# Attention with sinks and windows, then a gated long convolution, on one core: a third of the transform table copied by sign, turns as integers, the first evacuations in halves, and a new written-out order

## The chip, the cores and the metric

The kernel runs on one core of one Trainium2 chip. The metric is the device time of one execution in microseconds (us): 197.66 us is the median of three runs of the kernel before (197.52 to 197.74). A core has a matrix engine (PE), a vector engine (DVE), a scalar engine (ACT), GpSimd (POOL) and SyncE (SP), which here does nothing but issue DMAs. Each engine has an instruction queue of its own and takes it in order. PSUM holds what PE writes; here it is four pairs of banks, called slots 0 to 3.

## The reference

```python
def _attn_ref(q, k, v, is_retrieval, n_sink, window):     # 4 x 8 heads, 768 positions, head size 64
    scores = scale * np.matmul(q, k.transpose(0, 1, 3, 2))
    ...                                    # retrieval heads: causal; the others: causal and (sink or window of 64)
    scores = np.where(mask[None, :, :, :], scores, -1000000000.0)
    a = np.exp(scores - np.max(scores, axis=-1, keepdims=True))
    a = a / (np.sum(a, axis=-1, keepdims=True) + 1e-09)
    return np.matmul(a, v)

def _moe_ref(x, w_proj, filter_fft, w_out):               # x: 4 x 768 x 512, the heads side by side
    proj = x @ w_proj
    x1, x2, x3 = proj[..., :D], proj[..., D:2 * D], proj[..., 2 * D:]
    X2 = np.fft.rfft(x2, n=S, axis=1)
    H = np.fft.rfft(filter_fft, n=S, axis=0)[None, :, :]
    x2_conv = np.fft.irfft(X2 * H, n=S, axis=1)
    return (x1 * x2_conv * x3) @ w_out
```

## The kernel before

The 32 heads are worked on as 16 pairs `n` (four pairs for each of the four batches `b`). The transform is done as matmuls with a table `G` of cosines and sines, over 384 frequencies in three segments of 128 columns (segment 2 holds 64 cosines and 64 sines of the upper frequencies); `Gi` is its transpose.

Nothing is scheduled by a compiler. Each step is a small function under a name, and the string `ORDER` at the head of the file lists the names one after another; that list is the order of every engine's queue, the DMA issues of SP included. `@2` behind a name gives the PSUM slot, `/v`, `/s` and `/p` send a step that several engines can do to DVE, ACT or POOL. A step waits on semaphores for its inputs and for the buffer that it overwrites, and everything behind it on its engine waits too.

The names that matter here:

- `lq lk lv`: loads of a pair's q, k, v (L515, L527; 384 KB each, three buffers each). `cq ck cv`: casts to bf16. `T`: transposes, on PE for pairs 0 to 5 (L550), by DMA for pairs 6 to 15 (L560). `E`: copies PE's transposes out of PSUM into `qkT`.
- `sc n.c`: scores of chunk `c` (L574), `ex`: their exponentials on ACT (L593). `CHUNKS` says which 128 x 128 blocks (key block, query block) make a chunk. The two heads of a pair lie on partitions 0 to 63 and 64 to 127, so a score matmul uses half the rows of the array. `sb`: a bias added by a matmul, for the first four pairs (L587); the others are masked on DVE (`mk`, L603).
- `vf`: a masked copy of v (`v_far`, L541). `at`: probabilities times v (L612). `rec`, `nm`: normalization on DVE (L622, L627).
- `f`, `S`, `Se`: the two half sums, the transform (L640) and its copy out of PSUM. `tn`, `te`: the turned attention output (`xT`).
- `X`, `Xe`, `pa pb pc`: projection of the spectrum (L681) and its product with the filter; `c`, `ce`, `cv b.cb`: the inverse transform (L742); `x1`, `x3`, `xs`, `g`, `y`: the other two projections (L717) and the gates; `o`, `oe`, `st`: the output projection (L769), its copy and its store. `lw0 lw1 lw2` and `lwo`: weight loads, issued on POOL (L414, L419). `lw1` is the part that `X` reads.
- The table: `turns`, `angle`, `wrap` turn position times frequency into a fraction of a turn between -1/2 and 1/2 (three DVE steps for each of three row blocks, 384 columns wide); `size` takes its magnitude; `sin1 sin2 cos1 cos2` write `G` on ACT; `sin0` loads the sine's table ahead. `blank` are matmuls on zeros before there is work. `lret`, `heads0` to `heads2`: which heads are of which kind. `alt` writes one column of `G` on POOL.

The casts, copies and the steps in the table have one helper each, so many instructions carry the helper's line (L180 DVE, L182 POOL, L184 ACT).

Of the kernel before, what the change touches and what calls it, by code (L numbers as in the profile page):

```python
# [19 lines left out]
    [(0, 0), (0, 1), (0, 2), (0, 3)],  # L20
    [(4, 4), (4, 5), (0, 4), (0, 5)],
    [(1, 1), (1, 2), (1, 3), (1, 4)],
    [(3, 3), (3, 4), (3, 5)],
# [23 lines left out]
sc3.0@3 sc3.3@2 f02/v sb3.0 vf3/v sb3.3 ex3.0 T4.1@0 scales T4.0 F2.0 ck5/p E4.1/v ex3.3 S2.0@3 cq6/p H2.2/s
E4.0/v S2.1 at3.1@2 H2.0/s Se2/v tn2@0 at3.0 H2.1/s te2/v cv4/p sc4.1@3 rec3 lq7 sc4.2@0 nm3 F0.1@1 ex4.2
F0.0 f03/v ex4.1 f13/v tn3@0 cq5/v T5.1@2 H0.0/v T5.0 S3.0@3 te3/v E5.0/s S3.1 H0.2/v E5.1/s x10.0.0@0
H0.1/v Se3/s x10.0.1 H0.3/v x10.1.0@2 H0.4/v xs0.0/s cv5/p lv6 kinds sc4.3@3 sc4.0@1 ex4.3 sc5.1@0 x10.1.1  # L50
ex4.0 mask1 x30.0.0@3 xs0.1/v lk8 ex5.1 x30.0.1 mask0 sc4.5@2 g0.0 sc4.4@1 ex4.5 X0.1.0@0 ex4.4 mask2 mk4.1
sc5.0@3 sc5.2@2 ex5.0 sc5.4@1 mk4.0 X0.1.1 mask6 ex5.2 x10.3.1@3 Xe0.1/v vf5/s x10.3.0 ck6/p F1.1@2 xs0.3/v
ex5.4 F1.0 T6 mask3 sc5.5@3 vf4/v H1.0/s sc5.3@1 cq7/p x30.1.0@0 mk4.2 lq8 ex5.5 x30.1.1 lv7 ex5.3 X0.2.1@3
mk5.2 H1.1/s at4.1@1 mk5.0 H1.2/s X0.2.0 ck7/s mk5.1 g0.1 cv6/s at4.0 T7 Xe0.2/s at5.1@2 mask4 vf6/p rec4
at5.0 nm4 ck8/s sc6.4@3 rec5 sc6.2@0 f04/v ex6.4 lq9 x10.2.0@1 nm5 x10.2.1 lk9 ex6.2 mask7 mask5 sc6.5@2
cq8/p sc6.1@3 xs0.2/v ex6.5 x30.2.0@0 ex6.1 f15/p mk6.2 sc6.0@1 sc6.3@2 T8 x30.2.1 ex6.0 X0.0.0@3 f05/v
ex6.3 g0.2 sc7.3@1 sc7.1@2 mk6.0 ex7.3 sc7.5@0 X0.0.1 mk6.1 ex7.5 tn4 f14/v S4.0@1 ex7.1 cv7/v sc7.4@0
Xe0.0/v tn5 vf7/p S4.1 ex7.4 S5.1@2 Se4/v cq9/p sc7.0@3 sc7.2@0 ex7.0 S5.0 ck9/v at6.1@1 mk7.2 ex7.2 T9
at6.0 mk7.0 Se5/s sc8.4@3 mk7.1 sc8.0@0 hB ex8.0 rec6 at7.0@2 sw0.1 nm6 sw0.0 at7.1 ex8.4 hA f06/v f16/p
sc8.5@0 lv8 sc8.3@1 rec7 ex8.5 S6.0@3 tn6 nm7 ex8.3 sc8.2@0 S6.1 f17/v ex8.2 f07/v tn7 S7.1@1 Se6/v S7.0  # L60
pa0.1 sc9.2@0 Se7/s sc9.4@3 lk11 sc9.0@2 pa0.0 ex9.2 X1.1.1@1 mk8.2 Gi ex9.4 pb0.1 X1.1.0 pc0.1 ex9.0
X1.0.0@0 mk8.1 X1.2.1@3 Xe1.1/s lq10 pa0.2 cv8/v sc8.1@2 sc9.1@1 pb0.2 vf8/p ex8.1 X1.2.0 pc0.2 X1.0.1 lk10
Xe1.2/s x11.1.1@2 ex9.1 mk8.0 x31.1.1@3 pb0.0 ck11/p x11.1.0 mk9.0 lq11 x31.1.0 xs1.1/s at8.1@1 Xe1.0/s g1.1
at8.0 x11.0.0@2 pc0.0 lv9 rec8 x11.0.1 nm8 x31.0.1@3 xs1.0/v f18/p lv10 sc9.5@1 sc9.3@0 ex9.5 x31.0.0 f08/p
cq10/s c0.1.0@1 g1.0 x11.2.1@2 ex9.3 c0.1.1 ck10/s mk9.1 c0.0.0@0 ce0.1/s mk9.2 T10 x11.2.0 cq11/p ce0.0/s
cv0.1.0 c0.3.1@3 xs1.2/s cv0.1.1 c0.3.0 T11 y0.1 x31.2.1@1 cv9/p ce0.3/v x31.2.0 cv0.3.0 vf9/p lv11 S8.1@2
g1.2 lq12 S8.0 c0.0.1 cv10/p cv0.3.1 Se8/s at9.1@1 cv0.0.0 lwo y0.3 sc10.3@2 sc10.2@3 ex10.3 cv0.0.1 at9.0
lk12 vf10/v ex10.2 x30.3.1@0 rec9 nm9 sc10.4@2 sc10.0@3 ex10.4 x30.3.0 y0.0 f19/p c0.2.0@1 ex10.0 g0.3 tn8
c0.2.1 f09/p sc10.5@2 ce0.2/v sc11.4@3 ex10.5 S9.1@0 cv0.2.0 ex11.4 cv11/p S9.0 tn9 cv0.2.1 x11.3.0@2 pa1.1
Se9/s sc11.5@3 y0.2 lk13 sc11.3@1 ex11.5 x11.3.1 vf11/v ex11.3 sc11.1@3 mk11.2 sc10.1@0 ex11.1 o0.1.0@1  # L70
xs1.3/v o0.0.0 ex10.1 mk10.1 sc11.0@2 sc11.2@3 mk10.0 o0.2.0@0 ex11.2 mk10.2 o0.2.1 o0.3.0 ex11.0 mk11.1
at10.0@3 cq12/s mk11.0 at10.1 ck12/s o0.3.1 rec10 at11.0@2 nm10 oe0.3/s T12 at11.1 f110/v f010/p o0.4.0@3
rec11 nm11 o0.0.1 sw1.0 o0.5.0 sw1.1 f011/v o0.1.1 S10.1@2 f111/v oe0.1/v S10.0 ck13/p S11.0@0 Se10/s S11.1
pb1.1 st0.1 o0.4.1 lq13 Se11/s pc1.1 sc12.0@2 lv12 sc12.4@1 o0.5.1 pa1.0 ex12.4 tn11 X2.1.1@0 pb1.2 ex12.0
X2.1.0 pa1.2 X2.0.0@1 Xe2.1/s tn10 pc1.2 X2.0.1 oe0.5/s pb1.0 lk14 sc12.5@0 pc1.0 sc12.2@2 Xe2.0/s c1.0.1@3
cq13/v c1.0.0 ex12.5 T13 c1.1.0@1 ex12.2 ce1.0/v cv12/p c1.1.1 cv1.0.0 c1.3.1@0 vf12/p ce1.1/s cv1.0.1 lq14
X2.2.1@2 cv1.1.0 lv13 cv1.1.1 c1.3.0 y1.0 sc12.3@1 sc12.1@3 y1.1 ex12.3 X2.2.0 ce1.3/v ex12.1 mk12.2
x12.1.0@1 lq15 cv1.3.1 Xe2.2/s x12.1.1 ck14/v x12.0.1@3 cv1.3.0 xs2.1/s y1.3 sc13.3@0 sc13.2@2 ex13.3
sc13.5@1 mk12.0 x12.0.0 mk12.1 ex13.2 x31.3.1@0 x31.3.0 ex13.5 cq14/v xs2.0/s at12.1@2 g1.3 T14 sc13.0@1
sc13.1@3 mk13.1 ex13.0 sc13.4@0 cv13/p at12.0 st0.5 ex13.1 lk15 c1.2.1@1 rec12 vf13/p nm12 lv15 c1.2.0  # L80
ex13.4 x12.3.0@3 ce1.2/v x12.3.1 sw2.1 cq15/s f012/v cv1.2.1 x32.0.1@0 cv1.2.0 xs2.3/s mk13.2 sc14.4@2
sc14.5@1 sc14.1@3 mk13.0 ex14.5 x32.0.0 ex14.4 pa2.0 at13.0@1 lv14 g2.0 at13.1 ex14.1 x12.2.1@2 rec13 y1.2
ck15/s x12.2.0 nm13 o1.1.0@3 T15 xs2.2/s pa2.2 sc14.3@1 sc14.0@0 mk14.2 sc14.2@2 ex14.0 o1.0.0 sw2.0 cv15/v
pb2.1 o1.0.1 ex14.2 o1.1.1 x32.2.1@0 oe1.1/v cv14/p ex14.3 x32.2.0 vf15/p o1.4.0@2 vf14/s st1.1 g2.2 tn13
o1.4.1 sc15.4@1 f113/v sc15.2@3 mk14.0 ex15.4 sc15.0@0 o1.5.0 st0.3 f013/v pa2.1 tn12 ex15.0 o1.5.1
x32.1.0@1 mk14.1 oe1.5/s x32.1.1 pb2.2 S13.1@0 g2.1 ex15.2 st1.5 S13.0 at14.0@2 pc2.2 Se13/s f112/v sc15.3@3
sc15.1@1 pb2.0 ex15.3 sc15.5@0 at14.1 pc2.1 ex15.1 S12.1@3 rec14 pc2.0 S12.0 ex15.5 c2.1.1@1 mk15.1 Se12/s
o1.3.0@0 mk15.0 c2.0.0@3 nm14 o1.3.1 ce2.0/s c2.1.0 mk15.2 tn14 o1.2.0 ce2.1/s o1.2.1 cv2.1.1 at15.1@2
oe1.3/s f114/v cv2.1.0 at15.0 f014/v c2.0.1 rec15 nm15 S14.1@0 c2.2.0@1 f015/v tn15 S14.0 f115/v c2.2.1
cv2.0.1 Se14/s S15.0@2 cv2.0.0 S15.1 ce2.2/s x32.3.0@3 Se15/v x32.3.1 y2.0 c2.3.1@2 y2.1 c2.3.0 cv2.2.1  # L90
X3.2.1@0 cv2.2.0 ce2.3/v X3.2.0 cv2.3.0 X3.1.1@1 cv2.3.1 Xe3.2/s y2.3 X3.1.0 sw3.0 sw3.1 X3.0.1@0 Xe3.1/s
st1.3 X3.0.0 pa3.1 x13.2.0@1 pa3.2 Xe3.0/s x13.3.0@2 pb3.2 x13.0.0@0 g2.3 x13.0.1 pb3.1 x13.1.1@3 xs3.0/s
y2.2 x13.3.1 pc3.2 x33.0.1@0 pb3.0 xs3.3/s x33.0.0 pa3.0 x33.2.1@2 g3.0 x33.2.0 pc3.0 x13.2.1 x33.1.0@0
xs3.2/s x13.1.0 x33.1.1 xs3.1/v o2.0.0@1 pc3.1 c3.1.0@3 g3.2 o2.1.0 o2.1.1 g3.1 o2.0.1 c3.0.1@2 oe2.1/s
# [20 lines left out]
def kernel(  # L115
# [13 lines left out]
    nc = tc.nc  # L129
# [709 lines left out]
```

## Time and profile before

| | |
|---|---|
| median of three runs | 197.66 us (197.52 to 197.74) |
| the profiled execution | 198.84 us, its span 197.1 us |
| granted TensorE clock | 0.996 |
| busy: PE, DVE, ACT, POOL | 183.9, 171.5, 143.2, 46.0 us |
| moved by DMA | 37.31 MB, 189 GB/s over the span |

The span runs from the first to the last instruction of the program; the profiled execution is 1.74 us longer than its span and 1.18 us longer than the median of the runs. A busy PE means that a matmul's modelled duration covers the time; matmuls overlap, so starts of successive matmuls tell more than busy time. The wait column of a row names what came last of what the instruction waited for.

### The profile page before, as it was taken

The numbers are of one execution on the slowest core, as the hardware profiler recorded it, in microseconds if no ns is written. First come the engines' busy times: TensorE is split into PE (matmuls) and PEld (weight loads), VectorE is DVE, ScalarE is ACT, GpSimd is POOL, SyncE is SP. The second block draws the span as 40 slices with busy tenths as digits, with TensorE's granted clock in tenths as the row PEclk, the third lists the DMA queues.
The fourth block names the chain that finished last, engine by engine and source line by source line (L and its number), as shares of the span: only waits on it lengthen the run. The fifth ranks groups of instructions, "written<-read, shape, count | busy, mean of one in ns | idle before, by whom it ended". The sixth has DMA issues, their size and how long they took to land.

```text
span 197.1 us, 4350 instructions
## 1 busy us (share of the span) xinstructions
PE 183.9 (93%) x1740; PEld 104.1 (53%) x1740; DVE 171.5 (87%) x300; ACT 143.2 (73%) x183; POOL 46.0 (23%) x68
## 2 busy tenths in 40 slices
PE   7689989999998999999995999999999999999990
PEld 2355665664573564566542744566547664555540
DVE  7988998998998999979976898988999986968950
ACT  4999989989998998756694859689889524512341
POOL 4422946213031320524531110313030000000000
PEclk9999999999999999999999999999999999999998
DMA  5999999999959669999999599999998221302346
GB/s 179 324 305 357 307 270 197 242 218 198 202 103 178 134 136 214 208 227 191 200 190 178 106 202 221 213 232 225 237 239 250 43 40 39 124 2 91 122 170 256
DMA packets 93782, 37.31 MB, mean 189 GB/s; under 512 B 84162, under 2 KB 89282, under 8 KB 93762
## 3 DMA queue, kind: packets, MB, share of 16 engines
q1 hardware_dynamic: 91650, 34.94, 80.3%
q0 software_dynamic: 2112, 2.10, 6.7%
q8 instruction: 13, 0.21, 0.5%
q14 instruction: 7, 0.06, 0.1%
HBM read 24.64 MB, written 6.29 MB: 157 GB/s over the span
## 4 chain that ended last, share of the span: by engine, by line
PE 54%; DMA 14%; DVE 14%; SPq 6%; ACT 5%; POOL 2%; issue 2%; POOLq 0%; ACTq 0%
PE x_ps L717 13%; PE out_ps L769 9%; DMA v_f<-in_v_dram 8%; PE X_ps L681 7%; PE att L612 6%; PE sc L574 6%; PE S_ps L640 5%; PE c_ps L742 5%; DMA qk_f<-in_k_dram 4%; SPq L515 3%; ACT pT L593 3%; DMA qkT<-qk_bf 2%; SPq L347 2%; PE F_ps L435 2%; DVE conv L753 1%
## 5 line engine op out<-in xcount | busy, mean ns | idle before, releaser
L593 ACT ACTIVATE pT<-sc 128x1024 bf16<-128x1024 f32 (+2 forms) x96 | 82.0, 918 | 12.4 <-PE sc L574 10.4
L717 PE MATMUL x_ps<-xT,wproj 128*128 128x384 bf16 x256 | 46.3, 326 | 0.0
L717 PEld LDWEIGHTS <-wproj 128*128 128x128 bf16 x256 | 24.0, 98 | 18.0 <-issue 1.8
L574 PE MATMUL sc<-qkT 64*128 64x512 bf16 (+3 forms) x256 | 26.8, 306 | 4.3 <-DVE x1s L180 2.6
L603 DVE TENSOR_TENSOR pT<-pT,mask 128x1024 bf16<-128x1024 bf16 x37 | 24.4, 685 | 1.1 <-ACT pT L593 1.0
L612 PEld LDWEIGHTS <-pT 128*128 128x128 bf16 x672 | 22.9, 97 | 4.1 <-issue 1.9
L769 PE MATMUL out_ps<-wout,gy 128*128 128x512 bf16 x96 | 24.1, 380 | 0.2 <-DMA wout<-in_moe_w_out_dram 0.2
L612 PE MATMUL att<-v_aug,pT 128*128 128x65 bf16 x352 | 24.0, 193 | 0.1
L681 PE MATMUL X_ps<-wproj,spectrum 128*128 128x512 bf16 x96 | 22.7, 379 | 0.1
L612 PE MATMUL att<-v_far,pT 128*128 128x65 bf16 x320 | 20.7, 193 | 0.4 <-DVE v_far L541 0.4
L574 PEld LDWEIGHTS <-qkT 64*128 64x128 bf16 x256 | 10.5, 94 | 18.6 <-issue 12.7
L742 PE MATMUL c_ps<-Gi,P 128*128 128x384 bf16 x96 | 18.9, 326 | 0.0
L640 PE MATMUL S_ps<-G,halves 128*128 128x384 bf16 x96 | 18.4, 326 | 0.1
L753 DVE TENSOR_TENSOR conv<-evs,c_ps 128x384 bf16<-128x384 f32 x32 | 16.6, 549 | 1.3 <-ACT evs L184 1.0
L182 POOL CAST v_aug<-v_f 128x768 bf16<-128x768 f32 x10 | 8.8, 881 | 36.9 <-DMA v_f<-in_v_dram 29.5
L627 DVE TENSOR_TENSOR attn<-att,rec 128x768 bf16<-128x768 f32 x16 | 15.3, 955 | 0.7
L541 POOL TENSOR_TENSOR v_far<-v_aug,vmask 128x520 bf16<-128x520 bf16 x9 | 9.9, 1096 | 25.0 <-DVE v_aug L180 15.4
L184 ACT COPY o<-out_ps 128x1024 f32<-128x1024 f32 (+1 forms) x10 | 8.9, 885 | 9.3 <-PE out_ps L769 9.3
L184 ACT CAST spectrum<-S_ps 128x768 bf16<-128x768 f32 x11 | 8.8, 804 | 8.3 <-PE S_ps L640 8.2
L769 PEld LDWEIGHTS <-gy 128*128 128x128 bf16 x96 | 8.9, 98 | 10.8 <-issue 1.5
L681 PEld LDWEIGHTS <-spectrum 128*128 128x128 bf16 x96 | 8.9, 98 | 10.7 <-issue 1.3
L184 ACT CAST X<-X_ps 128x1024 bf16<-128x1024 f32 x10 | 10.2, 1023 | 5.7 <-PE X_ps L681 5.6
(98 smaller groups left out, 249.1 us busy)
## 6 DMA issues: line engine op xcount, KB each, us to landing
qk_f<-in_q_dram SPq DMA_DIRECT2D x16, 384.0 KB, 5.7
qk_f<-in_k_dram SPq DMA_DIRECT2D x16, 384.0 KB, 6.1
v_f<-in_v_dram SPq DMA_DIRECT2D x16, 384.0 KB, 7.0
out_dram<-o SPq DMA_DIRECT2D x9, 512.0 KB, 3.2
filt<-in_moe_filter_fft_dram SPq DMA_DIRECT2D x1, 1536.0 KB, 8.1
wproj<-in_moe_w_proj_dram POOLq DMA_DIRECT2D x3, 512.0 KB, 8.7
out_dram<-o SPq DMA_DIRECT2D x6, 256.0 KB, 2.5
Xw<-X SPq DMA_DIRECT2D x8, 128.0 KB, 2.9
```

The costliest lines, as they stand in the source:

```text
L184: nc.scalar.copy(out=out, in_=in_)
L574: nc.tensor.matmul(sc[:, hh, m * 128:(m + cnt) * 128], lhsT=qkT(n)[rows, 1, j * 128:(j + 1) * 128], rhs=qkT(n)[rows, 0, i * 128:(i + cnt) ...
L593: nc.scalar.activation(out=pT(n)[:, :, c, 0:w], in_=held[f"sc.{n}.{c}"][:, :, 0:w], func=AF.Exp, scale=SCALE)
L603: nc.vector.tensor_mul(near, near, which)
L612: nc.tensor.matmul(att[:, hh, 65 * i:65 * i + 65], lhsT=pT(n)[:, hh, c, 128 * m:128 * m + 128], rhs=(v_far(n) if i >= j + 2 else v_aug(n)) ...
L627: nc.vector.tensor_mul(attn(n).rearrange("p i hh d -> p hh i d"), rows[:, :, :, 0:64], held[f"rec.{n}"][:, :, :, None].to_broadcast([128, ...
L640: nc.tensor.matmul(ps[:, r, 0:HS], lhsT=halves(n)[:, r, m, :], rhs=G()[:, r, m].rearrange("p s f -> p (s f)"), start=(m == 0), stop=(m == ...
L681: nc.tensor.matmul(ps[:, u, :], lhsT=spectrum(b)[:, cc, r, seg * 128:seg * 128 + 128], rhs=wproj()[:, cc, DM:2 * DM], start=(cc == 0), sto ...
L717: nc.tensor.matmul(ps[:, s, 0:HS], lhsT=wproj()[:, cc, part * DM + cb * 128:part * DM + (cb + 1) * 128], rhs=xT(b)[:, cc, s * HS:s * HS + HS],
L742: nc.tensor.matmul(ps[:, r, 0:HS], lhsT=P(b)[:, t, u, ch], rhs=Gi()[:, r, :, seg, :], start=(seg == 0), stop=(seg == 2))
L753: fn(conv[:, half * HS:half * HS + HS], held[f"evs.{b}.{cb}"], held[f"c_ps.{b}.{cb}"][:, 1, 0:HS])
L769: nc.tensor.matmul(ps[:, i % 2, :], lhsT=gy(b)[:, cb, i * 128:(i + 1) * 128], rhs=wout()[:, cb, :], start=(cb == 0), stop=(cb == NC - 1))
```

## The change

- `CHUNKS`: block (0, 3) goes from chunk 0 to chunk 3. Chunk 0 is 384 columns wide and chunk 3 has 512, in two runs.
- For pair 0, each copy of the transposes out of PSUM (`E0.0`, `E0.1`) is made in two halves, `E0.a.0` and `E0.a.1`, of 384 columns.
- The table: `fcol` is 256 wide; `turns` multiplies and writes an integer, `wrap` multiplies again and subtracts it; `angle` is gone as a step; `size` is 256 wide. `sin2` and `cos2` are gone: segment 2 of `G` is written by four steps `far`, copies of segments 0 and 1 in reverse order times a sign for each row, which `signs` (two POOL instructions) prepares.
- `ORDER` is another list: other places, other engines for some steps, another order of loads.

```diff
 CHUNKS = [
-    [(0, 0), (0, 1), (0, 2), (0, 3)],
+    [(0, 0), (0, 1), (0, 2)],
...
-    [(3, 3), (3, 4), (3, 5)],
+    [(3, 3), (3, 4), (3, 5), (0, 3)],
...
         @op(f"turns{m}")
-            vp().tensor_scalar(out=turns()[:, m], in0=angle()[:, m], scalar1=MAGIC, scalar2=None, op0=ALU.add)
+            vp().tensor_scalar(out=turns()[:, m], in0=fcol(), scalar1=tfrac()[:, m:m + 1], scalar2=None,
+                               op0=ALU.mult)
         @op(f"wrap{m}")
-            nc.vector.scalar_tensor_tensor(out=angle()[:, m], in0=turns()[:, m], scalar=MAGIC,
-                                           in1=angle()[:, m], op0=ALU.subtract, op1=ALU.subtract)
+            nc.vector.scalar_tensor_tensor(out=angle()[:, m], in0=fcol(), scalar=tfrac()[:, m:m + 1],
+                                           in1=turns()[:, m], op0=ALU.mult, op1=ALU.subtract)
...
+    @op("signs")
+        for p in range(2):
+            nc.gpsimd.tensor_scalar(out=signs()[:, p:p + 1], in0=par(), scalar1=4.0 * p - 2.0, scalar2=1.0 - 2.0 * p,
+                                    op0=ALU.mult, op1=ALU.add)
+            @op(f"far{p}{r}")
+                near = G()[:, r, :, p, 1:65] if r == 0 else G()[:, r, :, p, 0:64]
+                vp().tensor_scalar(out=G()[:, r, :, 2, 64 * p:64 * p + 64], in0=near[:, :, ::-1],
+                                   scalar1=signs()[:, p:p + 1], scalar2=None, op0=ALU.mult)
...
+                for half in range(2 if n == 0 else 1):
+                    @op(f"E{n}.{a}.{half}" if n == 0 else f"E{n}.{a}")
+                        rows = slice(64 * half, 64 * half + 64) if n == 0 else slice(0, 128)
+                        copy(qkT(n)[:, a].rearrange("d (p t) -> d p t", t=NT)[:, rows],
+                             held[turned(n, a)][:, a, 0:S].rearrange("d (t p) -> d p t", t=NT)[:, rows])
```

The beginning of the new list, and the stretches of it that the prediction follows:

```text
mblank tcol lq0 fcol1 tfrac blank0@0 table fcol0 lret ident turns0/v lk0 turns2/v par sin0 turns1/v lk1
ones0 wrap0 lq1 ones1 scales wrap1 lk2 wrap2 lq2 unit sin1 size lv0 quarter heads0 blank1@1 cos1 cq0.0/v
cq0.1/v code0 ck0.1/p T0.0@0 ck0.0/s heads1@1 code1 heads2 lq3 T0.1@2 E0.0.0/v blank2@1 E0.1.0/v code2
E0.1.1/v sc0.0@3 ck1/p lk3 E0.0.1/v ex0.0 bias0 sc0.1@0 sc0.5@2 bias1 sc0.3@3 lv1 ex0.1 cq1/v sb0.5 sb0.3
T1.1@1 bias2 bias3 ex0.5 ck2/p lfilt T1.0@0 E1.1/v ex0.3 sc0.2@2 sb0.2 cq2/p E1.0/v sc0.4@1 ex0.2 sb0.4
T2.1@3 lv2 vmask mask01 sc1.1@0 ex0.4 mask00 sc1.2@2 cv0/v sb1.1 T2.0 ex1.1 bias5 sc1.0@1 vf0/v sb1.0 sb1.2
mk0.0 ex1.0 lk4 sc1.3@0 sb1.3 parb bias6 ex1.2 signs at0.1@1 bias4 ck3/p E2.1/v at0.0 ex1.3 cq3/p sc1.4@2
...
T6 H0.0/v x10.0.0 mk4.0 ex5.4 S3.0@0 xs0.0/v cv5/p H0.1/s lq8 S3.1 x10.3.0@1 H0.2/s lw1 Se3/v H0.4/s x10.3.1
...
X1.0.1@0 cq11/s rec9 nm9 X1.0.0 ce0.3/s T11 pb1.2 S8.0@1 f09/p Xe1.0/s S8.1 cv0.3.0 lv10 cv0.3.1 x31.2.1@2
```

## The prediction

> **What bounds the kernel now.** I read the page first, then PE's waits, then the timeline of the first 20 us, then the chain around the one long stall.
>
> ```profile
> span 197.1 us, 4350 instructions
> ...
> PE 183.9 (93%) x1740; PEld 104.1 (53%) x1740; DVE 171.5 (87%) x300; ACT 143.2 (73%) x183; POOL 46.0 (23%) x68
> ...
> PE   7689989999998999999995999999999999999990
> ```
>
> PE is busy from one end to the other, but for the beginning, one hole in the 22nd slice (103 to 108 us) and the stores at the end. So a gain can come from three places only: useful matmuls that begin earlier, fewer stalls between them, or less time per matmul. DVE at 87% is a near second, and where PE waits, DVE is mostly the one named:
>
> ```profile
> PE sc L574 <- DVE x1s L180: 2.6, 2, 1.9
> PE sc L574 <- DVE xT L180: 0.7, 1, 0.7
> ```
>
> The beginning, from the timeline:
>
> ```profile
> 1.87 0.40 DVE L307 TENSOR_SCALAR angle<-fcol,tfrac 128x384 f32<-128x384 f32 x1
> ...
> 4.30 1.49 DVE L316 SCALAR_TENSOR_TENSOR angle<-turns,angle 128x384 f32<-128x384 f32 x3
> ...
> 8.18 0.94 DVE L180 COPY qkT<-qkT_ps 128x768 bf16<-128x768 bf16 x1
> 8.43 1.28 ACT L593 ACT_TABLE_LOAD   x1
> ...
> 9.17 0.72 PE L574 MATMUL sc<-qkT 64*128 64x512 bf16 x8 [0.46 <-DVE qkT L180]
> ...
> 9.72 7.53 ACT L593 ACTIVATE pT<-sc 128x1024 bf16<-128x1024 f32 x9
> ...
> 16.18 0.19 PE L612 MATMUL att<-v_far,pT 128*128 128x65 bf16 x1 [0.37 <-DVE v_far L541]
> ```
>
> The first scores wait for DVE's second full copy `E0.1` until 9.17; the first attention product runs from 16.18. The long stall, in the chain:
>
> ```profile
> 95.67 8.62 DMA v_f<-in_v_dram
> ...
> 104.41 0.84 POOL v_aug L182
> 105.27 0.70 DVE v_far L541
> 105.97 0.60 DVE pT L603
> 106.57 0.88 DVE x1s L180
> 107.50 0.61 PE sc L574 x4
> ```
>
> By the order the load is `lv11`: `vf11/v` stands on DVE behind POOL's cast, DVE stops for it, and PE loses 2.1 us by the starts of its matmuls. From 30 us on, the other gaps over 0.12 us come to 2.7 us.
>
> **Part 1, the start.** DVE takes 3.92 us (1.87 to 5.79) for nine steps 384 wide, 0.436 each. Six remain, 256 wide: 0.29 each if length is all, 0.436 if it is nothing, and no row has an integer output; I take 0.31, in all 1.9 us (1.75 to 2.6). They can begin at about 1.5, since two of the four iotas (0.17 us each) go. So `wrap` ends at 3.4 and `size` (0.76 x 2/3 = 0.5) at 4.0. ACT then needs `sin1` 0.84 and `cos1` 0.92; `sin2` and `cos2` (0.51 and 0.60) are gone. With `ck0.0` (0.51, k landed by about 5.4, as `lret` goes ahead of it) and the table load (1.28) ACT is free at 7.1, now 9.71. DVE: `heads0` 0.70, two casts 0.36 each, `code0` 0.48, `heads2` 0.28 after the tiny matmul, to 6.5; then `E0.0.0` and `E0.1.0` at 0.48 each (half of 0.94 and a bit), to 7.45. PE's wait for `sc0.0` is on `E0.1.0`, not on the other halves: 7.6 instead of 9.17.
>
> But DVE takes some of that back. Before `at0` it still owes two halves 0.96, four biases 1.33, `cq1` 0.5, `E1` 1.85, `vmask` 0.2, two masks 0.67, `cv0` 0.55 (now POOL's), a bias 0.33, `vf0` 0.70 and `mk0.0` 0.6: 7.7 us, so `at0` runs at 15.2, not 16.18. PE has then done more scores than before at that point, some 0.5 us. The four `far` are new on DVE: 192 elements lie between `vmask`'s 32 (0.17) and the half sums' 384 (0.44), so 0.26 each, 1.05 us together, while the table's steps save 2.3 (4.68 against 2.4). I take 1.3 us for the start: at least 0, at most 2.0.
>
> The order of loads does not stand against it: k1, q1, k2, q2, v0 instead of k1, q2, q1, v1, k2, v0. In the trace the first nine loads land at 4.0, 5.0, 7.2, 8.4, 9.5, 11.2, 12.4, 14.1 and 15.1; in the new order the same places give pair 1 complete at 8.4 (now 9.5) and v0 at 12.4 (now 14.1), both before DVE comes to them.
>
> **Part 2, `signs` on POOL.** Behind its two instructions stand `ck3`, `cq3`, `cv1` and `vf1`, and PE waits for `T3`. The nearest rows are far apart: the 128x1 iota `par` took 0.13, but `alt`, three elements and the same operation, this:
>
> ```profile
> 21.58 1.77 DVE L427 TENSOR_TENSOR fold<-filt 128x1536 bf16<-128x1536 f32 x1
> ...
> 21.71 1.71 POOL L342 TENSOR_SCALAR G<-par 128x3 bf16<-128x3 int32 x1
> ```
>
> It ended within 0.1 us of the DVE instruction beside it. I take 0.15 each, as no such long step lies beside `signs`; at 1.71 each POOL would reach `ck3` at about 18.6 and PE would lose up to 2 us at `T3`, all of the start's gain. [...]
>
> **Part 3, more switches on PE.** Two score matmuls of the two heads start 3 to 4 ns apart and run together, but leaving them is not free:
>
> ```profile
> 18.05 0.39 PE L574 MATMUL sc<-qkT 64*128 64x512 bf16 x2
> ...
> 18.37 0.39 PE L587 MATMUL sc<-bias,identity 128*128 128x256 bf16 x2
> ```
>
> From the pair to the next full-height matmul it is 0.32 us, where a 512-column matmul takes 0.216 start to start: 0.1 us lost. The way in costs the same (`x` to `sc`: 0.258 where 0.162 is usual). The old list has 46 groups of scores, the new one 51: 5 x 0.19 = 0.95 us. The split run of chunk 3 replaces 128 of chunk 0's columns and adds a pair's fixed 0.01 us in 16 pairs, 0.15. Together +1.1 us on the path, which nothing hides; the least is 0.15, if the switches fall into waits. [...]
>
> **Part 4, stalls from 30 us on.** A place in a list becomes a time by the PE work ahead of it: `x10.0.0` has 29.2 us ahead of it and ran at 41.0, so 11.8 are added, and 10.5 in the new list, after the start's gain. Work leaves DVE: by the rows, 4 `xs` (0.953), 5 `ce` (0.552), 3 `Se` (0.952), 3 `H` (about 0.73) and 4 `oe` (3.3 together) go to ACT, one `Xe` (1.22) comes back; with the smaller moves and the table DVE loses 14 us of row time and ACT gains 8.7. About 80% and 77% busy instead of 87% and 73%: the waits on DVE should shorten. I take 0.5 us off the 2.7. The long stall: between `lv11` and `vf11` on DVE lie 9.5 us of PE work in the old list, and landing and cast took 9.5 after an issue that was late. Now `vf11` is POOL's, and the tight load is `lv10` with `vf10/v`, 10.1 us of PE work apart, again beside `lwo`. With SP 2 us late again, 1.5 us would remain; SP is less pressed, as `T10` and `T11` stand 3.5 us apart, not 1.6. I take 0.5, so 1.6 off. Sum -2.1, from -4 (all gone) to +3 (new ones, see the rivals). The end is alike in both lists, the last copy on ACT (0.59) and a store: 0, give or take 0.2.
>
> **The sum.** -1.3 + 1.1 - 2.1 = -2.3 us. The profiled execution of 198.84 would be 196.5, its span 194.8; the median lies 1.18 below the profiled execution, so 197.66 becomes 195.4.
>
> **Rivals.** *The third weight load comes late* (slower). `lw1` now stands behind `cv5` on POOL, 8.9 us of PE work before `X0.1.1`; it was 14. Its landing took 8.7, so `X0.1.1` waits for any lateness of v5. `lv5` has 22.0 us of PE work ahead of it, so is issued at about 32.5; `X0.1.1` has 42.6, so it comes at 53.1 and `cv5` must be done by 44: it decides from a landing of 11 us. Before, v5 took 15.3 us behind two weight loads (25.72 to 40.98); with that, PE would lose some 4 us: 199.4. For it: DMA is full at that time. Against it: only one weight load lies ahead of v5 now, and about as many bytes, which would land it near 41. *The start and the stalls give nothing* (POOL held up at `signs`, or DVE owing as much later): -0.5 and -0.5, with +1.1 from the switches, 197.8. *The stalls go almost all*: -1.3 + 1.1 - 4 = -4.2, 193.5.
>
> **How the numbers follow.** My sum, 194.4 to 196.8: 0.47. Stalls gone, below 194.4: 0.15. Nothing gained, 196.8 to 198.2: 0.20. Late weight load, above: 0.18. Leaving a tenth at each end, the range is 193.7 to 198.8. What can be told from no change is about 0.2%, 0.4 us: faster (below 197.26) 0.70, same 0.08, slower 0.22.
>
> **What would show it.** First scores near 7.6 and `at0` near 15.2; `signs` under 0.4 us together; `lw1` landed before the first `X`; PE's hole near 105 under 1 us; DVE near 80%. If the first scores are early and PE's lead is gone by 30 us, part 1 is wrong; if a hole of over 2 us stands near 50 us, the first rival is right.

## The result, and the profile after

The changed kernel takes 196.70 us (196.37 to 197.14, four runs) where the kernel before takes 197.59 (197.23 to 197.74): a ratio of 0.9959, 95% interval 0.9934 to 0.9983, 0.9 us faster. I had forecast 195.4, 2.3 us faster. The direction and the range held, but the gain is 0.4 of what I said. Later runs on three chips gave 0.9990 (0.9959 to 1.0021), 0.9947 (0.9906 to 0.9988) and 0.9969 (0.9933 to 1.0004). These ratios leave out executions that lie far above their kernel's fastest (3, 4 and 2 of the changed kernel's 12 on each chip); the medians and highest times below hold all, and by the medians of all the changed kernel takes 197.66, 198.10 and 197.42 us there and the kernel before 197.51, 197.54 and 197.60, so that no gain is left.

The page of the changed kernel, its profiled execution 196.82 us:

```profile
span 195.1 us, 4387 instructions
...
PE 184.0 (94%) x1755; PEld 103.9 (53%) x1772; DVE 162.5 (83%) x286; ACT 150.5 (77%) x198; POOL 49.2 (25%) x71
...
PE   7799989999999989999999999999999999999990
```

PE has no hole in the 22nd slice any more. DVE is at 83%, not at the 80% that I worked out, ACT at 77% as worked out. The beginning, from the timeline:

```profile
2.35 1.26 DVE L311 SCALAR_TENSOR_TENSOR angle<-fcol,tfrac,turns 128x256 f32<-128x256 f32 x3
...
6.48 1.28 ACT L599 ACT_TABLE_LOAD   x1
...
7.76 0.34 PE L580 MATMUL sc<-qkT 64*128 64x384 bf16 x2
...
15.29 0.48 POOL L333 TENSOR_SCALAR signs<-par 128x1 f32<-128x1 int32 x2 [3.71 <-DVE par L258]
15.38 0.25 PE L618 MATMUL att<-v_aug,pT 128*128 128x65 bf16 x3
```

`wrap` ends at 3.6, the scores start at 7.76 (I said 7.6), `signs` take 0.24 us each (I said 0.15). So the start went as worked out up to the scores. The first attention product stands at 15.38 (I said 15.2), but in the kernel before it ran from 15.56, and not from 16.18 as I read:

```profile
15.56 0.25 PE L612 MATMUL att<-v_aug,pT 128*128 128x65 bf16 x3
```

The row at 16.18 is the first product with `v_far`; in the changed kernel that one runs from 15.46. To find the rest I added up, for each profile, the time between the starts of successive PE steps beyond what the same steps take one behind the other. I call this sum PE's stalls; time lost in a stretch at a lower clock counts in it. Up to 30 us it is 8.71 us before and 7.32 after; from 30 us on it is 9.50 and 8.69. The table at the end of the experiments has it for all profiles that matter.

### The profile page after: what moved, and what is told of

Same layout as the page of the kernel before. It is cut to its first block, busy times and chain, and to the rows that moved or that the text cites. A ratio compares the mean times of both kernels' runs of the same rounds, so it can differ in the third digit from the quotient of the medians.

```text
span 195.1 us, 4387 instructions
## 1 busy us (share of the span) xinstructions
PE 184.0 (94%) x1755; PEld 103.9 (53%) x1772; DVE 162.5 (83%) x286; ACT 150.5 (77%) x198; POOL 49.2 (25%) x71
## 4 chain that ended last, share of the span: by engine, by line
PE 68%; DVE 13%; DMA 7%; ACT 5%; issue 3%; POOL 1%; POOLq 0%
PE x_ps L723 16%; PE out_ps L775 10%; PE X_ps L687 9%; PE att L618 8%; PE c_ps L748 8%; DMA v_f<-in_v_dram 7%; PE sc L580 7%; PE S_ps L646 6%; ACT pT L599 4%; DVE qkT L180 2%; DVE pT L609 2%; DVE attn L633 1%; DVE gy L737 1%; DVE fold L427 1%; PE qkT_ps L554 1%
## 5 line engine op out<-in xcount | busy, mean ns | idle before, releaser
L609 DVE TENSOR_TENSOR pT<-pT,mask 128x1024 bf16<-128x1024 bf16 x37 | 27.6, 766 | 3.1 <-ACT pT L599 2.8
L580 PE MATMUL sc<-qkT 64*128 64x128 bf16 (+3 forms) x288 | 27.4, 290 | 2.0 <-DVE qkT L180 0.8
L182 POOL CAST qk_bf<-qk_f 128x768 bf16<-128x768 f32 (+1 forms) x17 | 15.2, 896 | 30.5 <-DMA qk_f<-in_k_dram 21.8
L775 PE MATMUL out_ps<-wout,gy 128*128 128x512 bf16 x87 | 22.4, 379 | 0.4
L687 PE MATMUL X_ps<-wproj,spectrum 128*128 128x512 bf16 x90 | 22.1, 379 | 0.7 <-ACT spectrum L184 0.3
L580 PEld LDWEIGHTS <-qkT 64*128 64x128 bf16 x288 | 10.7, 94 | 16.8 <-issue 10.6
L184 ACT COPY o<-out_ps 128x1024 f32<-128x1024 f32 (+1 forms) x14 | 11.2, 835 | 9.3 <-PE out_ps L775 7.7
L184 ACT CAST X<-X_ps 128x1024 bf16<-128x1024 f32 x9 | 9.1, 1012 | 8.3 <-PE X_ps L687 8.1
L640 POOL TENSOR_TENSOR halves<-attn 128x384 bf16<-128x384 bf16 x10 | 10.0, 1006 | 20.3 <-DVE attn L633 13.2
L184 ACT CAST x1s<-x_ps 128x768 bf16<-128x768 f32 x14 | 11.3, 804 | 4.1 <-PE x_ps L723 3.9
```

The costliest lines, as they stand in the source:

```text
L182: nc.gpsimd.tensor_copy(out=out, in_=in_)
L184: nc.scalar.copy(out=out, in_=in_)
L580: nc.tensor.matmul(sc[:, hh, m * 128:(m + cnt) * 128], lhsT=qkT(n)[rows, 1, j * 128:(j + 1) * 128], rhs=qkT(n)[rows, 0, i * 128:(i + cnt) ...
L609: nc.vector.tensor_mul(near, near, which)
L687: nc.tensor.matmul(ps[:, u, :], lhsT=spectrum(b)[:, cc, r, seg * 128:seg * 128 + 128], rhs=wproj()[:, cc, DM:2 * DM], start=(cc == 0), sto ...
L775: nc.tensor.matmul(ps[:, i % 2, :], lhsT=gy(b)[:, cb, i * 128:(i + 1) * 128], rhs=wout()[:, cb, :], start=(cb == 0), stop=(cb == NC - 1))
```

## The experiments

Theory A: the long stall near 105 us, of which I took off 1.6 us, belonged to the one profiled execution of the kernel before. Theory B: it is in every execution, and new small stalls ate the gain. Theory C: the start's gain is given back. Later two more came up. D: POOL's steps hold DVE's back. E: whether POOL's load of `wout` or the transpose `T11` of pair 11 gets to the DMA queues first decides some microseconds in the changed kernel.

**The kernel before, once more** (`e1_before_again`, no edit).

> The kernel before, unchanged, profiled and timed once more. Theory A (my sum was made against one slow profiled execution): its profiled execution of 198.84 us lay 1.2 us above the median because the stall of 2.1 us near 105 us (v of pair 11, landing 8.62 us) is larger there than in most executions. A expects a profiled time near 197.5 and under 1.0 us of stall near 105. Theory B (the stall is in every execution, and new small stalls between 50 and 75 us of the changed kernel ate what its removal gave) expects about 2 us of stall near 105 again, in a profile near its own median. Both: median 197.6, ratio 1.000.

Measured: 197.92 us (196.71 to 198.74), ratio 1.0008 (0.9983 to 1.0034); the profiled execution took 197.88, its span 196.2. The timeline near 105 us:

```profile
94.77 0.80 POOL L418 DMA_DIRECT2D wout<-in_moe_w_out_dram  x1
94.82 0.38 SPq L526 DMA_DIRECT2D v_f<-in_v_dram  x1
...
101.93 1.09 POOL L181 CAST v_aug<-v_f 128x768 bf16<-128x768 f32 x1 [1.85 <-DMA v_f<-in_v_dram]
...
103.06 0.70 DVE L540 TENSOR_TENSOR v_far<-v_aug,vmask 128x520 bf16<-128x520 bf16 x1 [0.72 <-POOL v_aug L181]
...
105.64 0.60 PE L573 MATMUL sc<-qkT 64*128 64x512 bf16 x4
```

The same load, v of pair 11, is issued at 94.82 and has landed by 101.93, so that DVE waits 0.72 us for POOL's cast and not 2.52, and PE's scores follow with no wait shown. In this execution PE loses 0.94 us near 103 (for `wout`) and 1.0 us near 140 instead. The stalls up to 30 us are 8.47, from there 8.82, together 0.92 less than in the first profile; its span is 0.9 less. That is what theory A expects: the first profile lay above the median, and this stall, which the second has not, is the largest difference between them. The second is one execution too.

**One letter for the long stall** (`e4_vf11_pool`).

```diff
-... x11.3.1 vf11/v ex11.3 ...
+... x11.3.1 vf11/p ex11.3 ...
```

> The kernel before with one letter changed: the far copy of v of pair 11 runs on POOL (about 1.1 us there, 0.70 on DVE), so DVE no longer stops behind POOL's cast near 104 us. The attention product of pair 11 stands 3.7 us of PE work later, so POOL's copy is in time. Theory B and my sum expect the long stall to go: -1.4 to -1.9 us, median 195.7 to 196.2. Theory A expects 0 to -0.5, median 197.1 to 197.6, since most executions have little of that stall.

Measured: 197.36 us (196.74 to 198.12), ratio 0.9972 (0.9945 to 0.9999), about 0.5 us (0 to 1.1). The stall near 105 is gone (0.11 us between 105 and 110), and a median execution has about a third of it to give, not the 1.6 us of my sum. That is the end of what theory A allows, and far from B.

**The two lists crossed** (`e2_new_start`, `e3_new_rest`).

```diff
 e2: changed code
-ORDER = changed list
+ORDER = changed list up to nm2, then what is left in the order of the old list
 e3: old code
-ORDER = old list
+ORDER = old list up to ex3.5, then what is left in the order of the changed list
```

> The changed kernel's code, and its list up to nm2 (some 30 us of the span), then the old list's order for all that is left. Groups of scores: 48 (old 46, changed 51). By my terms: start -1.3, chunk 3 split +0.15, two more groups +0.4, the long stall near 105 as in the old list: -0.75, so 196.8. Theory C (the start's gain is given back where DVE and POOL owe the work) expects 197.4 to 197.9, with PE's lead over the old kernel gone between 16 and 40 us. Theories A and B both expect 196.6 to 197.0.

> The old code (old table, whole first evacuations, old chunks) and the old list up to ex3.5 (some 30 us), then the changed list's order for all that is left. Groups of scores: 51, five more than before. By my terms: switches +0.95, stalls -2.1: -1.15, so 196.4. Theory A expects the stalls to give only what a median execution has of them, 0.5 or so: +0.4, near 198.0. Theory B expects -2.1 from the old stalls, +1.5 from new ones between 50 and 75 us and +0.95 from the switches: +0.35, also near 198.0, but with over 1.2 us of stalls above 0.3 us between 50 and 75 us in its trace. Theory C expects 196.4 to 196.9.

Measured: 199.78 (ratio 1.0095, 1.0060 to 1.0129) and 203.79 (1.0297, 1.0250 to 1.0344). Both miss every theory. The traces show why: the seam costs. In the first, PE loses 1.05 us twice, at 27.9 and 29.3, for ACT's copies of `S` and of the turned output, without which the next steps have no slot; in the second 5.6 us go between 30 and 45 us: PE sits idle there for 2.4 us, 2.1 of them for ACT's exponentials, and the granted clock is 0.72, 0.50 and 0.92 in the three windows from 34 to 40 us. Neither list carries the other's debts, and these two runs tell nothing of the start alone.

**Whole first evacuations, and the old table** (`e6_whole_evac`, `e7_old_table`, beside the changed kernel again as `e5_after_again`).

```diff
 e6
-... E0.0.0/v blank2@1 E0.1.0/v code2 E0.1.1/v sc0.0@3 ck1/p lk3 E0.0.1/v ...
+... E0.0/v blank2@1 E0.1/v code2 sc0.0@3 ck1/p lk3 ...
 e7
-... turns0/v ... cos1 ... signs ... far00/v ... far01/v ... far10/v ... far11/v ...
+... angle0/v turns0/v ... sin2 cos2 cos1 ...              # 384 columns wide, old code of the table
```

> The changed kernel, unchanged, beside its variants on the same chip. The first runs gave a ratio of 0.9959. Theory A (what I forecast too much is the stall near 105 us, which the first profile of before had and a second one did not) expects 0.994 to 0.997 again, and a profile whose stalls to 30 us are 1.1 to 1.3 us less than those of the kernel before (7.3 against 8.1 to 8.7), while those after 30 us differ by less than 0.7. A rival (chance in the first four runs) would have the ratio at 0.988, where my forecast was.

> The changed kernel with the first two evacuations of qkT whole, in the places of the first two halves. DVE does the same work, but the first scores start 0.95 us later (8.7, not 7.76). If my account of the start holds (at0 is set by what DVE owes before it, and ACT's exps fill the time before), the first scores are worth less than they are early: +0.3 us to +0.9, I take +0.6 against the changed kernel. If the halves are worth nothing, 0 to +0.2; if ACT is the chain from the first exp on, the full +0.95.

> The changed kernel with the old table of sines: nine steps 384 wide on DVE, four iotas, sin2 and cos2 on ACT ahead of Exp, no signs and no copies by sign. DVE's table takes 3.9 us, not 2.2, and ACT has 1.1 us more before its table load. The first scores should start near 9.4 (7.76 changed, 9.17 before). My account expects +1.2 to +1.8 us against the changed kernel, less the 0.9 us of far copies that DVE is spared near 20 us: +0.6 to +1.4. If the start of the scores is set by the loads and not by DVE, 0 to +0.3.

Measured: the changed kernel 197.66 us (196.33 to 200.71), its ratio of 0.9990 above the 0.994 to 0.997 that theory A expected; with whole evacuations 199.38 (198.87 to 201.80); with the old table 203.23 (202.27 to 205.59). For the whole evacuations the scores start at 8.15, later by 0.3 us than beside it, the attention at 15.35 against 15.20, and the stalls to 30 us are the same, 7.74 against 7.75: by the trace, one profile of each, the halves are worth nothing in the end, less than the 0.3 to 0.9 us expected. That DVE's debt before `at0` decides there fits this and is not shown by itself. The 1.7 us come from another place: PE waits 2.1 us near 99 for the DMA transpose of q and k, `T11`. The old table cost far more than I expected: the first scores start at 10.08 and the first attention at 20.38, stalls to 30 us are 12.20 (three matmuls on zeros take 1.20 us from 8.95, where they take 0.81 with whole evacuations). An order that was planned for a short table cannot take the long one; so this says what the table is worth in this list, not that it brought 5 us.

The second profile of the changed kernel has what the first had not, a stall of 1.85 us at 97.85, for `g1.2`; the old-table kernel has it too.

**Four moves at the stalls of the first profile** (`e8_four_moves`).

```diff
-... pb0.1 sc6.1@3 x30.2.1 ex6.1 X0.2.1@0 g0.2 ...    -... vf6/v ...    -... sc3.5@1 sc3.3@0 ...    -... mk9.0 c0.1.1 cv9/s g1.0 ...
+... sc6.1@3 x30.2.1 ex6.1 X0.2.1@0 g0.2 pb0.1 ...    +... vf6/p ...    +... sc3.3@0 sc3.5@1 ...    +... c0.1.1 cv9/s g1.0 mk9.0 ...
```

> The changed kernel with four moves, each at a stall of its trace: pb0.1 behind g0.2 (PE lost 0.52 us near 58 for gy), vf6 on POOL (0.45 near 54, where DVE had waited 1.06 us for POOL's cast), sc3.3 ahead of sc3.5 (0.76 near 28.5), mk9.0 behind g1.0 (0.48 near 88). Theory B (the new small stalls are on the path and have eaten the gain) expects -1.0 to -1.8 us against the changed kernel. Theory A expects the same sign and less, -0.3 to -1.0, since the waits behind them on other engines come next. If PE's stalls there are covered by what DVE or ACT owes later, 0 or worse.

Measured: 197.44 (195.69 to 202.73), ratio 0.9968 (0.9933 to 1.0003), 0.2 us under the changed kernel beside it: inconclusive. Three of the four stalls, at 54, 58 and 88, are absent from the second profile of the changed kernel too, without any move; they were that execution's own. The stall for `g1.2`, near 98 in the second profile, is there again with 1.80 us. With theory B's stalls gone by themselves and the time the same, B falls as I put it; a new stall there is, but it is this one.

**Two half sums from POOL to DVE** (`e9_halves_dve`; `e10_with_moves` adds two of the four moves; `e12_after_control` is the changed kernel beside them).

```diff
-... S8.0@1 f09/p Xe1.0/s ... sc10.2@1 f19/p x31.2.0 ...
+... S8.0@1 f09/v Xe1.0/s ... sc10.2@1 f19/v x31.2.0 ...
```

> The changed kernel with the two half sums of pair 9 on DVE instead of POOL (0.35 us each there, 0.93 to 1.2 on POOL). In the second profile of the changed kernel y0.3, a DVE step of 0.55 us elsewhere, took 2.69 us from 94.83, beside POOL's issue of wout, a half sum and two steps of v, and PE lost 1.85 us behind it. Theory D (POOL's steps hold DVE's back, and that is where the forecast stalls stayed) expects y0.3 at 0.55 to 1.2 us, PE's loss there under 0.5, and the median 0.8 to 1.6 us below the changed kernel's. Theory A alone (the profile of before was slow, nothing else) expects no more than 0.3 us.

> As the last, with pb0.1 behind g0.2 and mk9.0 behind g1.0, the two moves of the four that put nothing more on POOL. Each takes 0.68 us of DVE work out from ahead of a gate that PE waited for, 0.52 and 0.48 us in the first profile of the changed kernel. Expected: another 0.4 to 0.9 us below the last; 0 if the work behind it is late in its place.

> The changed kernel, as the measure of the first two on the same chip: a ratio of 0.994 to 1.000 to the kernel before, and y0.3 at 1.9 or 2.7 us in its profile again.

Measured: 202.45 (200.73 to 205.91), 201.97 (198.83 to 203.97) and 198.10 (195.99 to 200.73). A clear miss, and the most telling one. `y0.3` is near 0.55 us again, as theory D has it, but PE now waits 3.86 us near 99 for the DMA transpose, 4.55 in the other. With one step less ahead of it (`f09`; `f19` stands behind), POOL issued `wout` at 92.5 and not at 93.8 to 95.2 as in the profiles of the changed kernel; `T11`, issued by SP at 93.3, landed at 103.2, where it lands at 97.4 to 99.4 in those. The control has `y0.3` at 1.93 us, one of the two values expected. Theory E came from this.

**Nine more groups of scores** (`e11_split_groups`, the kernel before).

```diff
-... sc13.3@0 sc13.2@2 ex13.3 sc13.5@1 mk12.0 x12.0.0 ...
+... sc13.3@0 sc13.2@2 ex13.3 x12.0.0 sc13.5@1 mk12.0 ...       # and eight like it, pairs 12 to 15
```

> The kernel before with nine groups of scores of pairs 12 to 15 cut in two: one matmul step that stood behind the group stands ahead of its last score, so PE goes nine more times from half-row to full-height matmuls and back. Nothing else changes. At 0.19 us each: +1.7 us, in a region where PE has under 0.1 us of stalls per us. If the switches cost nothing, 0, and the +0.95 us of my sum for five groups was wrong.

Measured: 198.81, ratio 1.0053 (1.0021 to 1.0084), 1.05 us or 0.12 each (0.05 to 0.18). The switches cost, at some two thirds of the 0.19 that I took. The moved steps can cost waits as well: in this run's profile PE waits 0.90 us near 145 for a transpose, where the first profile of the kernel before has 0.22. So 0.12 is not shown to be the switch alone.

**The issue of `wout` later, and earlier** (`e13_wout_later`, `e15_wout_earlier`; `e14_later_moves` adds two moves; `e16_after_control` is the changed kernel beside them).

```diff
 e13
-... Se8/s lv12 lwo y0.3 ... sc10.2@1 f19/p x31.2.0 ...
+... Se8/s lv12 y0.3 ... sc10.2@1 f19/p lwo x31.2.0 ...
 e15
-... S8.0@1 f09/p ... lv12 lwo y0.3 ...
+... S8.0@1 lwo f09/p ... lv12 y0.3 ...
```

> The changed kernel with one word moved: POOL issues wout (lwo) behind the half sum f19, near 96.9 us, not 95. Theory E (whether wout or the transpose T11 gets to the DMA queues first decides some 2 to 4 us) expects T11 to land near 98.2 to 99.4 every time, no executions above 198.5, and a median of 196.0 to 197.0, a wait for wout of up to 1 us at the first output product included. Theory D (DVE beside POOL decides) expects the spread as in the control, since POOL has the same steps beside y0.3 and the next product.

> The changed kernel with the same word moved the other way: wout ahead of the half sum f09, near 92.5 us. Theory E expects T11 to land at 101 to 103.5 every time, PE to wait 2 to 4.5 us for it near 99, and a median of 199 to 201. Theory D expects less than the control, since the issue of wout no longer stands beside y0.3: -0.5 us or so.

> The changed kernel on the same chip. Theory E expects two groups of times, near 196.2 and at 198 to 200.7, as before, and a median between the last and the first of this call.

> As the last, with pb0.1 behind g0.2 and mk9.0 behind g1.0. In the last profiles of the changed kernel these two gates cost PE 0 to 0.5 us each, so 0 to -0.8 us against the last: 195.5 to 196.8. This is the version that the experiments point to, and it should be 0.5 to 1% below the kernel before.

Measured: later 196.29 us (195.09 to 199.46, eleven of twelve under 197.3); earlier 203.28 (202.27 to 204.32); the changed kernel 197.42 (195.38 to 200.04); the kernel before 197.60. One word, moved by a few places either way, is worth -1.1 and +5.9 us by the medians. The timeline of the earlier one:

```profile
91.78 0.80 POOL L422 DMA_DIRECT2D wout<-in_moe_w_out_dram  x1
92.50 5.45 SPq L565 DMA_TRANSPOSE qkT<-qk_bf  x1
...
104.02 0.50 PE L579 MATMUL sc<-qkT 64*128 64x384 bf16 x2 [5.22 <-DMA qkT<-qk_bf]
```

and of the later one:

```profile
92.26 1.96 SPq L565 DMA_TRANSPOSE qkT<-qk_bf  x1
93.15 2.07 POOL L639 TENSOR_TENSOR halves<-attn 128x384 bf16<-128x384 bf16 x2 [1.52 <-DVE attn L632]
94.54 1.09 DVE L766 TENSOR_TENSOR conv<-conv,x1s 128x768 bf16<-128x768 bf16 x1
...
95.16 0.81 POOL L422 DMA_DIRECT2D wout<-in_moe_w_out_dram  x1
...
98.60 0.34 PE L579 MATMUL sc<-qkT 64*128 64x384 bf16 x2
```

In the first, `wout` is issued 0.72 us ahead of `T11`: SP is held 5.45 us in issuing the transpose, and the scores wait 5.22 us. In the second, `wout` comes 2.9 us behind it, SP is held 1.96, and the same scores wait for nothing. This is theory E, for an early `wout`. These times show that an early `wout` holds the transpose up, and not how.

The earlier one is dearer than expected (199 to 201): behind its pause the granted clock falls too, to 0.50 from 104 to 106 us, and 1.7 us of clock are missing; the later one has one execution over the 198.5 that I gave as its bound. The control's twelve times lie spread, and not in two groups.

The changed kernel stands close to the edge between the two. In its four profiles `wout` comes 1.9 to 2.1 us after SP has begun on `T11`, which SP takes 1.95 to 2.25 us to issue, and `T11` is not held up. With whole evacuations `wout` came 1.81 us after (92.47 and 94.28), SP took 3.86 us, and PE lost its 2.1. So theory E is at work in no profile of the changed kernel; whether it is in the executions above 198.2 us, of which none was profiled, is not shown. The fourth profile, beside the two above:

```profile
93.83 0.80 POOL L423 DMA_DIRECT2D wout<-in_moe_w_out_dram  x1
94.07 2.69 DVE L767 TENSOR_TENSOR conv<-conv,x1s 128x768 bf16<-128x768 bf16 x1
...
94.65 0.92 POOL L640 TENSOR_TENSOR halves<-attn 128x384 bf16<-128x384 bf16 x1
95.51 0.83 POOL L182 CAST v_aug<-v_f 128x768 bf16<-128x768 f32 x1
...
99.13 0.81 PE L723 MATMUL x_ps<-xT,wproj 128*128 128x384 bf16 x4 [1.77 <-DVE gy L737]
```

Here `T11` got through (landed at 97.40), and theory D shows instead: `y0.3`, 0.55 us by its median of four, runs from 94.07 to 96.76, until 0.42 us after POOL's cast has ended; the step behind it takes 1.54 where it took 0.68 a little earlier; and PE waits 1.77 us for the gate behind both. When `wout` is issued later, `y0.3` takes 1.09 us and ends 0.41 us after POOL's half sums, and nothing waits.

Whether this stall comes goes with the landing of v of pair 11, which POOL casts next. In the fourth profile v had landed at 95.10, before POOL's half sum ended, so the cast followed at once. In the third it landed at 97.21:

```profile
95.14 1.93 DVE L767 TENSOR_TENSOR conv<-conv,x1s 128x768 bf16<-128x768 bf16 x1
...
95.72 0.92 POOL L640 TENSOR_TENSOR halves<-attn 128x384 bf16<-128x384 bf16 x1
...
97.35 1.00 POOL L182 CAST v_aug<-v_f 128x768 bf16<-128x768 f32 x1 [0.71 <-DMA v_f<-in_v_dram]
```

POOL pauses, `y0.3` is through after 1.93 us, and PE has no stall over 0.2. The seven profiles in which these steps of POOL follow `wout` in this order all agree: with the cast at once `y0.3` takes 2.69 or 2.70 us and PE waits 1.7 to 1.8 (second, fourth, four moves, old table), with the cast 0.46 to 1.07 us later it takes 1.93 and PE waits 0.16 at most for that gate (first, third, whole evacuations). An earlier landing goes with a slower execution here. No run moves the landing alone, and since a later `wout` takes away both meetings, with `T11` and with `y0.3`, its 1.1 us are not split between E and D.

The version with the two moves as well took 195.91 us (195.59 to 197.44, seven runs), ratio 0.9932 (0.9898 to 0.9967); the later `wout` alone 0.9926 (0.9899 to 0.9953). The two can't be told apart, and both beat the kernel before by 0.7%. Against the changed kernel on the same chip the medians are 1.1 to 1.5 us lower, though the intervals of the ratios overlap a little (0.9933 to 1.0004 for the changed kernel). Over 198.5 us lie one of the 19 executions of the two versions, one of the changed kernel's 12 beside them, and ten of its 36 on all three chips.

PE's stalls by profile, worked out as said above, in us:

| profile | to 30 us | from 30 us on | largest stall between 90 and 110 us |
|---|---|---|---|
| before, first | 8.71 | 9.50 | 2.10, v of pair 11 |
| before, second | 8.47 | 8.82 | 0.94, `wout` |
| changed, first | 7.32 | 8.69 | none over 0.2 |
| changed, second | 7.75 | 9.20 | 1.85, `g1.2` behind `y0.3` |
| changed, third | 8.15 | 7.00 | none over 0.2 |
| changed, fourth | 7.33 | 9.79 | 1.84, the same |
| `wout` later | 7.77 | 6.78 | 0.25, `wout` |
| `wout` earlier | 7.67 | 13.71 | 5.38, `T11` |

## Why the prediction was right in direction and wrong in size

- **The step that failed is the stall term of part 4, -2.1 us.** Measured, it is -0.5: from 30 us on the changed kernel's four profiles have 8.67 us of stalls in the mean, the two of before 9.16. The term was wrong at both of its ends. On the side of before, the 2.1 us were in one profiled execution; the second had none of it there, and taking its cause away gave 0.5 us by the ratio, where the term had 1.6. I had written down that the profiled execution was 1.18 us above the median, and then treated this as an even offset: I took the stall off and took the 1.18 off as well. The two were largely the same microsecond (0.92 us less stalls in the second profile, 0.9 us less span): from profile to profile the change gave 198.84 to 196.82, -2.0, but the changed kernel's first profile lies 0.12 above its median, not 1.18. On the side of after, I had seen that a new tight place would stand near 100 us beside `lwo`, and put the late load `lv10` there with 0.5 us. The place was right and the load wrong: what PE waits for there is `g1.2` behind `y0.3`, which POOL's steps hold on DVE. Two of four profiles lose 1.8 us by it, the others nothing. `T11`, which an earlier `wout` holds up, is late in none of the four.
- With that place out of the way the term is not simply right. From 30 us on, 6.78 us are left with `wout` later and 7.00 in the third profile of the changed kernel, 2.2 to 2.4 less than in the mean of before; but the first profile, which has no stall there either, keeps 8.69, with stalls of some 0.5 us near 54, 58 and 88. What the planned order saves without the collision lies between 0.5 and 2.4 us, and is open.
- **Start, -1.3 us:** right up to the first scores, size a bit large; the attention's start was a misread row, as shown above. To 30 us the changed kernel's four profiles have 7.64 us of stalls in the mean, against 8.59 in the two of before: -0.95. The share that I gave to the halves is not seen (with whole evacuations the stalls by 30 us are the same, one profile of each).
- **Switches, +1.1 us:** a little too high. At 0.12 us for a group, five groups and 0.15 for chunk 3 are 0.75; the 0.15 was not measured. With the measured sizes the sum is -0.95 + 0.75 - 0.5 = -0.7 us, beside the 0.9 measured at first (0.3 to 1.3).
- **`signs`, 0.15 us each:** 0.24, and `alt`, the row of 1.71 us that was my upper bound, took 0.21 us in its new place, with no `fold` beside it:

```profile
19.21 0.21 POOL L346 TENSOR_SCALAR G<-par 128x3 bf16<-128x3 int32 x1
```

- **DVE near 80%:** 83%. Its row time fell by 9.0 us (171.5 to 162.5), not by 14. The 37 mask multiplies alone take 3.0 us more:

```profile
L609 DVE TENSOR_TENSOR pT<-pT,mask 128x1024 bf16<-128x1024 bf16 x37 | 27.6, 766 | 3.1 <-ACT pT L599 2.8
```

  They took 685 ns each before. Adding up, for all DVE steps that run over 0.25 us beyond the usual time of their kind, what they take beyond it gives 4.6 and 5.4 us in the two profiles of before and 8.7, 10.6 and 8.2 in the first three of the changed kernel. I had put a price on POOL's neighbourhood for `signs` only, and taken DVE's durations for all moved steps from rows with another POOL beside them. In the second profile of the changed kernel a mask multiply, which has two inputs, took 1.31 us beside POOL's cast and 0.69 alone, and a mask step with one input took 1.72 us beside POOL and 0.41 alone.
- **Rivals.** The late weight load `lw1` did not come: no profile shows PE waiting for `wproj`. It was near: `lw1` landed at 51.51 and `X` began at 52.67 in the first profile, at 52.25 and 53.21 in the second. "The start and the stalls give nothing", 197.8, is near what the changed kernel takes on other chips (197.4 to 198.1), but by another cause than I gave, since the start does give its part. "Stalls almost all gone" is not seen.
- What would have shown it beforehand: the order of the list around `lwo`. `T11` stands a few words ahead of it on another queue, and nothing but POOL's work decides which comes first; and `lwo`, `f19` and `cv11` follow one another on POOL where DVE has `y0.3`, on which `g1.2` and PE wait.

## What to carry to other kernels

A stall that hangs on a DMA's landing belongs to an execution, not to a kernel, until a second profile shows it (here 2.10 us in one, none in the next): do not take it off a sum whose profile already lies above the median by as much. In a list by hand, look for pairs of transfers on different queues whose order nothing fixes, above all a large one issued by POOL beside one that PE will wait for, and put the large one behind: here the 512 KB of `wout` 0.72 us ahead of `T11` made 203.28 us, and 2.9 us behind it 196.29. And a step sent to POOL to relieve DVE can hold DVE's neighbour step for as long as POOL works on: `y0.3`, which reads SBUF alone, took 2.69 us here, not 0.55.

## What the runs showed of the hardware

- PE's granted clock fell behind some pauses of about 2 us and more, to 0.50 in the lowest window of 2 us, and not behind others. In the fourth profile of the changed kernel the pause was 1.8 us; from the table of windows (busy times and counts of each engine, then the granted clock, the DMA share and GB/s):

```profile
98.00:100.00 2.00, 0.87 (x6) 0.38 (x5) 1.97 (x4) 0.47 (x1) 0.00 (x0) 1.00 1.16 180
100.00:102.00 2.00, 2.00 (x12) 0.60 (x10) 1.70 (x4) 1.02 (x2) 0.00 (x0) 0.59 1.27 267
102.00:104.00 2.00, 2.00 (x14) 0.72 (x12) 2.00 (x4) 1.31 (x2) 0.42 (x1) 0.55 0.63 121
104.00:106.00 2.00, 2.00 (x17) 1.09 (x12) 2.00 (x3) 1.94 (x3) 1.68 (x2) 1.00 1.45 237
```

  The missing clock of the two middle rows is (0.41 + 0.45) x 2 = 1.7 us. Beside the second profile, which has the same pause and keeps its clock, the same steps run 0.77 us ahead just behind the pause (99.13 and 99.90) and 0.75 behind at the next transform (104.83 and 104.08): 1.5 us, so this stall cost nearly twice its length. The missing clock is 1.7 us as well for whole evacuations (pause 2.2), the half sums on DVE (3.9) and `wout` earlier (5.4), and 3.4 us for the half sums with two moves (4.5). The second profile of the changed kernel, with 1.85 us of pause, and the first of before, with 2.1, kept the clock at 1.00. What decides is not shown.
- DVE steps that read SBUF alone did not slow down in proportion beside POOL here: they ended, as a rule, as if they had stood still until POOL's step was through. In the six profiles of the kernel before and the changed kernel, steps that take 0.35, 0.55, 0.69 and 1.77 us alone ended 0.21, 0.42, 0.54 and 1.62 us after it, each some 0.14 us less than its own length. POOL steps one behind the other held them through, as `y0.3` above with its 2.69 us. A short case, a half sum on DVE beside one on POOL, in the first profile of the changed kernel:

```profile
91.41 1.09 POOL L640 TENSOR_TENSOR halves<-attn 128x384 bf16<-128x384 bf16 x1 [4.79 <-DVE attn L633]
91.64 1.07 DVE L640 TENSOR_TENSOR halves<-attn 128x384 bf16<-128x384 bf16 x1
```

  The products `conv<-evs,c_ps`, which have an input in PSUM, were not held: of 41 that began while POOL was at work on a step, in the same six profiles, none took longer than the usual 0.55 us. Of 22 mask multiplies, which read SBUF alone and take 0.69 us alone, 21 took longer.
- SP was held 5.45 us in issuing `T11` when `wout` had gone ahead of it, and 1.95 to 2.25 us in the changed kernel's four profiles; the next load on SP was issued from 98.01, where it was issued from 94.28 with `wout` later. Other transposes hold SP for 1.2 to 5.7 us in those profiles and one, at 39.74 in the first, for 11.12; `wout` is not their cause, as it comes only once, near 95 us.
